# A hand-planned linear-attention and MLP kernel: other ready times for loaded rows, a last tile in two column halves, table copies as planned tasks

## The chip, the cores and the metric

The kernel runs on one core of a Trainium2 chip. Its time is the device time of one launch in microseconds (us). The core has five engines that each work through their own instructions in order: TensorE (PE in the profile; its weight loads are PEld), VectorE (DVE), ScalarE (ACT), GpSimd (POOL) and SyncE (SP). Sixteen DMA engines move data between memory and the core; the kernel starts transfers from the queues of SyncE, ScalarE and GpSimd. TensorE writes to PSUM, eight banks of 2 KB per partition; everything else lies in SBUF.

## What is computed

A recurrent linear attention (RWKV-5) for 4 sequences of 768 steps with 8 heads of 48 columns, then a normalised two-layer MLP with a residual, over 384 columns:

```python
def _attn_ref(r, k, v, w, u):
    state = np.zeros((B, H, D, D), dtype=np.float32)
    for t in range(S):
        cur = np.einsum('bhd,bhe->bhde', u[None] * kt, vt)
        y[:, :, t] = np.einsum('bhd,bhde->bhe', rt, state + cur)
        state = w[None, :, :, None] * state + np.einsum('bhd,bhe->bhde', kt, vt)

def _moe_ref(x, g_ln, w_ch1, w_ch2):
    xn = (x - mu) / np.sqrt(var + 1e-06) * g_ln
    ch = np.maximum(xn @ w_ch1, 0.0) @ w_ch2
    return x + ch
```

All inputs and the output are float32. The hidden layer has 1536 columns.

## The kernel before

The 4 x 768 rows are cut into 24 tiles of 128 rows, six for each sequence. Inside a tile the recurrence is written as matmuls. Row t of r is scaled by w^t and row t of k by w^-t, so that decayed scores are a plain product, masked to the lower triangle; the state that goes from a tile to the next is multiplied by w^128. The scaling factors are three tables, Fr (two halves, for the even and the odd rows that r's load puts side by side) and Fk.

For tile i, with the planner's task names: sck scales k and scr scales a pair of r tiles (L366, L369), TK and TR transpose them on TensorE through the one PSUM bank "tr" (L384, L399), kT and rT copy them out (L388, L404), q is their product (L415) and cc the bonus sums by matmul (L442), copied out by cp (L453). "at" are the scores (L422), A the masked scores (L432), vc the cast of v to bf16 (L375), Vb the bonus term (L457), kv, S and Z the state (L473, L488, L497), y the output of the attention (L513, L525), x that with its row sum (L538). xn, sq and rs centre the rows and make the scale of the normalisation (L556, L565, L576). ln or a DMA transpose turns xn (L602, L610), lc copies it out of PSUM for the first eight tiles (L614). Then come the MLP's up matmuls (L627) for a group of one tile (the first six) or two tiles, re, the rectifier on ScalarE or VectorE (L641, L643), the down matmuls dn (L654), ot, the final sum (L664), and st, the store (L675). dn of a tile has 12 matmuls of 384 columns in three tasks of four; they add up in bank "o", or in one of the two "hp" banks for the odd ones of the last four tiles.

Which engine does what and in which order is set by a planner that runs when the kernel is built (class Planner, L22). Each task has an engine, a cost in us, tasks that it needs, buffers that it takes and gives, a priority, and perhaps other engines with their costs (alt). The planner holds a clock for each engine. Again and again it takes the task that can start first, on the engine on which it would end first, and writes its instructions there. A load has a planned landing, made from one planned DMA clock: it starts at most 3 us before that clock, moves it by `load`, and lands `lands` (1.9 us unless given) later. The planned times are used for the order alone; on the chip an instruction waits for its data, and everything behind it on its engine waits with it.

Line 74 of the planner adds SLK to ready times of TensorE's tasks, and SLK is 0.0, so it adds nothing. PACE = 4.4 holds the scaling of k: from the seventh tile on it is planned no sooner than 35 us + 4.4 us for each tile (L730).

The start is written by hand: the powers of w are made on VectorE by scans, transposed on TensorE (L308), and the three tables copied by ScalarE (L310). To the planner this is three tasks without instructions, "scan", "Fr" and "Fk", that only stand for the time. While TensorE has nothing to do in the first stage, keep_warm (L266) writes matmuls without use into bank "o" for the gap that the planner sees (L816 to L820).

The loads go in the order of `seq` (L697), with three loads of w1 behind the ninth and three of w2 behind the fourteenth. There are 7 buffers each for k, v and the cast v, 4 for pairs of r, 2 for scaled r, 4 for scaled k, 8 for the hidden layer hT, 11 for x.

Of the kernel before, what the change touches and what calls it, by code (L numbers as in the profile page):

```python
# [9 lines left out]
FP32 = mybir.dt.float32  # L10
# [7 lines left out]
SLK, SLT = 0.0, 35.0  # L18
# [3 lines left out]
class Planner:  # L22
# [24 lines left out]
    def order(self, patience=0.0, spread=0.0, seed=0):  # L47
# [15 lines left out]
        while todo:  # L63
            best = None
            for t in todo:
                data = t["after"]
                ok = True
                for n in t["needs"]:
                    d = self.by_name[n]
                    if d["end"] is None:  # L70
                        ok = False
                        break
                    lag = 0.0 if d["eng"] == t["eng"] else self.LAG[d["eng"]]
                    if t["eng"] == "PE" and d["eng"] not in ("PE", "") and eng_at["PE"] > SLT:
                        lag += SLK
                    data = max(data, d["end"] + lag)
# [50 lines left out]
def kernel(  # L127
# [16 lines left out]
    L = P  # L144
# [158 lines left out]
    LH = L // 2  # L303
    for j in range(3):
        fps = ps_h.tile([P, 512], FP32, name="hp") if j < 2 else ps.tile([P, 512], FP32, name="y")
        for kc in range(CK):
            src = T2[:, kc] if j == 2 else T[:, kc, j : 2 * L : 2]
            nc.tensor.transpose(out=fps[:, kc * P : (kc + 1) * P], in_=src, identity=ident_f[:])  # L308
        src = fps[:, :C].rearrange("p (h d) -> p h d", h=H)
        nc.scalar.copy(out=Fr[:, j] if j < 2 else Fk[:], in_=src)  # L310
# [89 lines left out]

    def evacuate_r(i, eng):
        e, c = divmod(i, 2)
        rT_t[i] = trp.tile([P, HP, P], BF16, name="rT", bufs=NRT)
        (eng.copy if eng is nc.scalar else eng.tensor_copy)(  # L404
            out=rT_t[i][:].rearrange("p q (t j) -> p q j t", j=2),
            in_=tp_t[e][:, :, c * LH : (c + 1) * LH].rearrange("p (j q) t -> p q j t", j=2),
        )
# [43 lines left out]
    def bonus_copy(i):  # L451
        cc_t[i] = sb2.tile([P, H], FP32, name="cc")
        nc.scalar.copy(out=cc_t[i][:], in_=s_t[i][:, C : C + H])  # L453
# [158 lines left out]
    def ln_evacuate(i):  # L612
        g, j = tile_group[i]
        nc.scalar.copy(out=xT_t[g][:, :, j * P : (j + 1) * P], in_=tp_t[i][:, :CK, :])  # L614
# [3 lines left out]
    def up(g, m):  # L618
        gw = group_len[g] * P
        nf = 512 // gw  # L620
        if m == 0:
            hT_t[g] = sb3.tile([P, FK, GW], BF16, name="hT", bufs=NH)
# [54 lines left out]

    plan = Planner(
# [5 lines left out]
    add("scan", "DVE", 5.65, None, pri=99)  # L684
    add("Fr", "ACT", 5.9, None, pri=99)
    add("Fk", "ACT", 0.65, None, needs=["Fr"], pri=99)
# [36 lines left out]
    for i in range(NT):  # L723
# [8 lines left out]
        if not half:  # L732
            add(f"scrb{e}", "", 0.0, None, [], [("scr", e, 1)], pri=p0)
            for t in range(2):
                add(f"scr{e}{t}", "POOL", 1.1, lambda g, e=e, t=t: scale_r(e, t, g), [f"r{e}", "Fr", f"scrb{e}"], [],
                    [("r", e)], pri=p0, alt=[("DVE", 0.7)])
            add(f"TR{e}", "PE", 0.46, lambda e=e: transposes_r(e), [f"scr{e}0", f"scr{e}1"], [("tr", ("r", e), 2)],
# [7 lines left out]
        else:  # L745
            add(f"kT{i}", "SP", 1.25, lambda i=i: transpose_k_by_dma(i), [f"sck{i}"], [("kT", i, 2)], [("sck", i)], pri=80,
                load=0.67, lands=3.0)
# [11 lines left out]
        add(f"cp{i}", "ACT", 0.2, lambda i=i: bonus_copy(i), [f"cc{i}"], [("cc", i, 1)], [("s", i)], pri=p0 + 1)  # L759
# [32 lines left out]
        if i < LNP:  # L792
            add(f"ln{i}", "PE", 0.18, lambda i=i: ln_transposes(i), [f"xn{i}", f"xT{g}"], [("tr", ("l", i), 1)],
                [("xn", i)], pri=p0 + 2)
            add(f"lc{i}", "ACT", 0.5, lambda i=i: ln_evacuate(i), [f"ln{i}"], [], [("tr", ("l", i))], pri=p0 + 2)
        else:
            add(f"lc{i}", "SP", 1.2, lambda i=i: ln_by_dma(i), [f"xn{i}", f"xT{g}"], [], [("xn", i)], pri=90, load=0.5, lands=3.0)
        for m in range(NM):
# [7 lines left out]
    for g, n in enumerate(group_len):  # L806
        for m in range(NU[g]):
# [3 lines left out]
                [f"lc{group_first[g] + j}" for j in range(n)] + [f"w1s{q}{kc}" for q in w for kc in range(CK)],  # L811
                [("hp", (g, m), 1)] + ([("hT", g, n)] if m == 0 else []), [("xT", g)], pri=-40, kind="u")
            add(f"re{g}_{m}", "ACT", 0.6, lambda e, g=g, m=m: relu(g, m, e), [f"up{g}_{m}"], [], [("hp", (g, m))], pri=30, alt=RA)
    pe_at = 6.1
# [39 lines left out]
```

## Time and profile before

| | |
|---|---|
| median of 13 runs | 158.27 us (156.98 to 160.22) |
| the profiled execution | 157.08 us |
| its span, first to last instruction | 155.3 us |
| granted TensorE clock, mean | 1.000 |
| TensorE busy | 146.4 us (94%) |
| VectorE busy | 119.1 us (77%) |
| ScalarE busy | 97.0 us (62%) |
| GpSimd busy | 85.8 us (55%) |
| moved by DMA | 25.46 MB, mean 164 GB/s |
| landing of the last v | 94.5 us |
| last attention matmul of the last tile (L525) | 122.6 us |
| last matmul | 151.5 us |
| last store: issue, landing | 152.21, 154.08 us |

The page of the profile is of that one execution. The 40 slices of a row each stand for 3.9 us, and a digit is the busy share in tenths. In the tables by stage each engine's busy us is followed by the number of its instructions, then come the granted clock, the share of the DMA engines and GB/s. In a timeline a line has start, duration, engine, line, operation, output and inputs, and in brackets how long the engine was idle before it and what ended that. In a list of waits a line has who waited for whom, us in total, how often, and the longest.

### The profile page before, as it was taken

The numbers are of one execution on the slowest core, as the hardware profiler recorded it, in microseconds if no ns is written. First come the engines' busy times: TensorE is split into PE (matmuls) and PEld (weight loads), VectorE is DVE, ScalarE is ACT, GpSimd is POOL, SyncE is SP. The second block draws the span as 40 slices with busy tenths as digits, with TensorE's granted clock in tenths as the row PEclk, the third lists the DMA queues.
The fourth block names the chain that finished last, engine by engine and source line by source line (L and its number), as shares of the span: only waits on it lengthen the run. The fifth ranks groups of instructions, "written<-read, shape, count | busy, mean of one in ns | idle before, by whom it ended". The sixth has DMA issues, their size and how long they took to land.

```text
span 155.3 us, 4634 instructions
## 1 busy us (share of the span) xinstructions
PE 146.4 (94%) x1851; PEld 114.7 (74%) x1851; DVE 119.1 (77%) x232; ACT 97.0 (62%) x217; POOL 85.8 (55%) x116
## 2 busy tenths in 40 slices
PE   5999999989999999999989989999999999999990
PEld 5889898867887667777758767787787777777650
DVE  5879999978898999999999879898989731101231
ACT  3568888867866577667858558676576554463100
POOL 7379697588729896785975939954442120000000
PEclk9999999999999999999999999999999999999999
DMA  4999999999999899899998977212121220111122
GB/s 94 235 239 336 353 195 287 367 226 214 243 222 214 207 234 226 192 231 172 227 222 178 204 175 157 78 30 76 50 55 51 80 73 3 51 55 51 51 101 101
DMA packets 75418, 25.46 MB, mean 164 GB/s; under 512 B 69632, under 2 KB 74246, under 8 KB 75398
## 3 DMA queue, kind: packets, MB, share of 16 engines
q1 hardware_dynamic: 72070, 23.21, 64.4%
q10 hardware_dynamic: 3232, 1.97, 4.2%
q8 instruction: 14, 0.23, 0.7%
q14 instruction: 6, 0.05, 0.1%
q0 software_dynamic: 96, 0.01, 0.0%
HBM read 18.88 MB, written 4.72 MB: 152 GB/s over the span
## 4 chain that ended last, share of the span: by engine, by line
PE 47%; DMA 21%; SPq 8%; DVE 7%; POOL 6%; issue 4%; ACT 4%; POOLq 0%; ACTq 0%
PE o L654 18%; PE hp L627 18%; DMA wst<-in_moe_w_ch_dram 11%; DMA v<-in_v_dram 10%; SPq L195 5%; PE hp L654 3%; DVE q L415 2%; PE at L422 2%; PE tr L399 2%; PE tr L384 1%; PE y L525 1%; POOL w_sb L350 1%; POOL Vb L457 1%; ACT kT L388 1%; DVE A L432 1%
## 5 line engine op out<-in xcount | busy, mean ns | idle before, releaser
L627 PE MATMUL hp<-xT,w_sb 128*128 128x256 bf16 (+1 forms) x540 | 57.6, 251 | 0.0
L654 PE MATMUL o<-w_sb,hT 128*128 128x384 bf16 x264 | 52.1, 326 | 0.0
L627 PEld LDWEIGHTS <-w_sb 128*128 128x128 bf16 x540 | 43.5, 98 | 7.2 <-DVE w_sb L350 0.2
L641 ACT ACTIVATE hT<-hp 128x512 bf16<-128x512 f32 x60 | 35.7, 598 | 19.1 <-PE hp L627 18.5
L654 PEld LDWEIGHTS <-hT 128*128 128x128 bf16 x288 | 26.2, 98 | 13.1
L664 DVE SCALAR_TENSOR_TENSOR ot<-o,rs,x 128x384 f32<-128x384 f32 x22 | 13.4, 610 | 22.5 <-PE o L654 22.5
L432 DVE TENSOR_TENSOR A<-at,mask 128x1024 bf16<-128x1024 f32 x24 | 29.1, 1214 | 0.5 <-PE at L422 0.5
L457 POOL TENSOR_TENSOR Vb<-v,cc 128x384 f32<-128x384 f32 x24 | 20.0, 835 | 11.2 <-ACT cc L453 11.2
L369 POOL TENSOR_TENSOR sc<-r,Fr 128x384 bf16<-128x384 f32 x18 | 20.2, 1134 | 6.3 <-ACT Fr L310 2.8
L366 POOL TENSOR_TENSOR sc<-k,Fk 128x384 bf16<-128x384 f32 x19 | 19.7, 1038 | 0.0
L388 ACT COPY kT<-tr 128x512 bf16<-128x512 bf16 x22 | 12.9, 586 | 5.5 <-PE tr L384 3.4
L565 ACT ACTIVATE sq<-x,sum 128x384 bf16<-128x384 f32 x24 | 14.6, 607 | 2.1 <-DVE x L538 2.1
L404 ACT COPY rT<-tr 128x512 bf16<-128x512 bf16 x17 | 11.8, 736 | 3.6 <-PE tr L399 2.3
L268 PE MATMUL o<-ident 128*128 128x128 bf16 x152 | 12.1, 233 | 1.6 <-DVE ident L243 1.6
L538 DVE SCALAR_TENSOR_TENSOR x<-y,Vb 128x384 f32<-128x384 f32 x24 | 13.1, 546 | 0.4 <-PE y L525 0.2
L268 PEld LDWEIGHTS <-ident 128*128 128x128 bf16 x152 | 9.9, 104 | 1.9 <-DVE ident L243 1.6
L422 PE MATMUL at<-rT,kT 48*128 48x128 bf16 x192 | 9.5, 219 | 1.2 <-ACT kT L388 1.1
L643 DVE TENSOR_SCALAR hT<-hp 128x512 bf16<-128x512 f32 x12 | 8.2, 687 | 2.0 <-PE hp L627 1.8
L525 PE MATMUL y<-vv,A 128*128 128x48 bf16 x192 | 8.8, 184 | 1.0 <-DVE A L432 1.0
L556 ACT ACTIVATE xn<-x,sum 128x384 bf16<-128x384 f32 x13 | 8.0, 615 | 2.6 <-DVE x L538 2.6
L497 DVE TENSOR_TENSOR Z<-S,WLZ 128x384 bf16<-128x384 f32 x11 | 9.4, 856 | 0.0
L422 PEld LDWEIGHTS <-kT 48*128 48x128 bf16 x192 | 5.4, 94 | 4.9 <-ACT kT L388 2.4
(87 smaller groups left out, 195.8 us busy)
## 6 DMA issues: line engine op xcount, KB each, us to landing
r<-in_r_dram SPq DMA_DIRECT2D x12, 384.0 KB, 4.7
k<-in_k_dram SPq DMA_DIRECT2D x24, 192.0 KB, 4.6
wst<-in_moe_w_ch_dram SPq DMA_DIRECT2D x6, 768.0 KB, 7.6
v<-in_v_dram SPq DMA_DIRECT2D x22, 192.0 KB, 4.0
out_dram<-ot SPq DMA_DIRECT2D x16, 192.0 KB, 3.3
out_dram<-ot ACTq DMA_DIRECT2D x8, 192.0 KB, 1.9
v<-in_v_dram ACTq DMA_DIRECT2D x2, 192.0 KB, 3.5
xT<-xn SPq DMA_TRANSPOSE x16, 3.0
```

The costliest lines, as they stand in the source:

```text
L268: nc.tensor.matmul(out=warm[:, :P], lhsT=ident[:], rhs=ident[:], start=True, stop=True)
L366: eng.tensor_tensor(out=k_bufs[i % NSC][:, :, :D], in0=k_t[i][:], in1=Fk[:], op=ALU.mult)
L369: eng.tensor_tensor(out=r_bufs[e % NSR][:, j, :, :D], in0=r_t[e][:, :, j * D : (j + 1) * D], in1=Fr[:, j], op=ALU.mult)
L388: (eng.copy if eng is nc.scalar else eng.tensor_copy)(out=kT_t[i][:], in_=tk_t[i][:, :HP, :])
L422: nc.tensor.matmul(out=at_t[i][:, par, p, :], lhsT=kT_t[i][p0 : p0 + D, p, :], rhs=rT_t[i][p0 : p0 + D, p, :], start=True, stop=True,)
L432: nc.vector.tensor_tensor(out=A_t[i][:].rearrange("p e q t -> p (e q) t"), in0=at_t[i][:].rearrange("p e q t -> p (e q) t"), in1=mask[:].u ...
L457: nc.gpsimd.tensor_tensor(out=Vb_t[i][:], in0=vf_t[i][:], in1=cc_t[i][:].unsqueeze(2).to_broadcast([P, H, D]), op=ALU.mult)
L565: nc.scalar.activation(out=sq[:], in_=x_t[i][:], func=ACT.Square, bias=sum_t[i][:], scale=-float(C), accum_out=sq_t[e][:, c : c + 1],)
L627: nc.tensor.matmul(out=hp[:, f * gw : (f + 1) * gw], lhsT=w1_sb[:, n, kc, fb * P : (fb + 1) * P], rhs=xT_t[g][:, kc, :gw], start=(kc == 0) ...
L641: nc.scalar.activation(out=out, in_=src, func=ACT.Relu)
L654: nc.tensor.matmul(out=o_t[i][:, :C], lhsT=hT_t[g][:, fk, j * P : (j + 1) * P], rhs=w2_sb[:, fk, :], start=(fk == 0), stop=(fk == FK - 1),)
L664: nc.vector.scalar_tensor_tensor(out=ot_t[i][:], in0=o_t[i][:, :C], scalar=rs_t[i // 2][:, i % 2 : i % 2 + 1], in1=x_t[i][:], op0=ALU.mult ...
```

## The change

There are five edits.

1. SLK, SLT go from 0.0, 35.0 to 3.0, 30.0, and the rule that they stand in is another one. It no longer looks at TensorE. Now any task with an engine that needs a load of the common kind (`lands` is 1.9: r, k, v, w1, w2) whose planned start is over 30 us is ready 3.0 us later than that load's planned landing.
2. The three tables are copied by planned tasks Fr0, Fr1 and Fk, each on ScalarE (0.5) or VectorE (0.48). Place-holders "first" and "rows0" stand for the time of ScalarE and GpSimd before, and tFr0, tFr1 and tFk for the ends of the transposes. scr of each half needs its own half of Fr.
3. The last tile's down matmuls are 2 x 12 of 192 columns, in two column halves with an "hp" bank each, the second after the first; each half has its own final sum and store.
4. cp (0.2 on ScalarE) may go to VectorE at 0.15, lc (0.5) at 0.36. TR needs the TK of the tile before, from the eleventh tile on.
5. A place-holder hTb takes the hidden layer's buffer as soon as a group's rows are there; before, the first up task took it. `up` makes the tile when it is first wanted. The place where the planner's clock of TensorE begins for keep_warm goes from 6.1 to 6.3. A `lands` of 5.0 in place of 3.0 is in a branch for tiles from KP = 24 on, of which there are none.

```diff
-SLK, SLT = 0.0, 35.0
+SLK, SLT = 3.0, 30.0
...
-                    if t["eng"] == "PE" and d["eng"] not in ("PE", "") and eng_at["PE"] > SLT:
+                    if d["load"] and d["lands"] == 1.9 and t["eng"] and d["start"] > SLT:
                         lag += SLK
...
-        fps = ps_h.tile([P, 512], FP32, name="hp") if j < 2 else ps.tile([P, 512], FP32, name="y")
+        tab.append(ps_h.tile([P, 512], FP32, name="hp") if j < 2 else ps.tile([P, 512], FP32, name="y"))
...
-        src = fps[:, :C].rearrange("p (h d) -> p h d", h=H)
-        nc.scalar.copy(out=Fr[:, j] if j < 2 else Fk[:], in_=src)
+
+    def copy_table(j, eng):
+        src = tab[j][:, :C].rearrange("p (h d) -> p h d", h=H)
+        (eng.copy if eng is nc.scalar else eng.tensor_copy)(out=Fr[:, j] if j < 2 else Fk[:], in_=src)
...
-        if m == 0:
+        if g not in hT_t:
             hT_t[g] = sb3.tile([P, FK, GW], BF16, name="hT", bufs=NH)
...
+    def down_half(h, m):
+        g, j = tile_group[NT - 1]
+        if m == 0:
+            oh_t[h] = ps_h.tile([P, 512], FP32, name="hp")
+        for fk in range(m * PM, (m + 1) * PM):
+            nc.tensor.matmul(
+                out=oh_t[h][:, :CH],
+                lhsT=hT_t[g][:, fk, j * P : (j + 1) * P],
+                rhs=w2_sb[:, fk, h * CH : (h + 1) * CH],
+                start=(fk == 0),
+                stop=(fk == FK - 1),
+            )
+
+    def finish_half(h):
+        i = NT - 1
+        oth_t[h] = sb2.tile([P, CH], FP32, name="oth")
+        nc.vector.scalar_tensor_tensor(
+            out=oth_t[h][:],
+            in0=oh_t[h][:, :CH],
+            scalar=rs_t[i // 2][:, i % 2 : i % 2 + 1],
+            in1=x_t[i][:, h * CH : (h + 1) * CH],
...
+    def store_half(h, eng):
+        b, c = divmod(NT - 1, NCH)
+        eng.dma_start(out=out[b, c * L : (c + 1) * L, h * CH : (h + 1) * CH], in_=oth_t[h][:])
...
-    add("scan", "DVE", 5.65, None, pri=99)
-    add("Fr", "ACT", 5.9, None, pri=99)
-    add("Fk", "ACT", 0.65, None, needs=["Fr"], pri=99)
+    add("scan", "DVE", 5.75, None, pri=99)
+    add("first", "ACT", 4.95, None, pri=99)
+    add("rows0", "POOL", 4.9, None, pri=99)
+    for j, (name, done, bank_) in enumerate((("Fr0", 5.45, "hp"), ("Fr1", 5.85, "hp"), ("Fk", 6.2, "y"))):
+        add(f"t{name}", "", done, None, pri=99, takes=[(bank_, ("t", j), 1)])
+        add(name, "ACT", 0.5, lambda e, j=j: copy_table(j, e), [f"t{name}"], gives=[(bank_, ("t", j))], pri=99 - j, alt=[("DVE", 0.48)])
...
-                add(f"scr{e}{t}", "POOL", 1.1, lambda g, e=e, t=t: scale_r(e, t, g), [f"r{e}", "Fr", f"scrb{e}"], [],
+                add(f"scr{e}{t}", "POOL", 1.1, lambda g, e=e, t=t: scale_r(e, t, g), [f"r{e}", f"Fr{t}", f"scrb{e}"], [],
...
-            add(f"TR{e}", "PE", 0.46, lambda e=e: transposes_r(e), [f"scr{e}0", f"scr{e}1"], [("tr", ("r", e), 2)],
+            add(f"TR{e}", "PE", 0.46, lambda e=e: transposes_r(e), [f"scr{e}0", f"scr{e}1"] + ([f"TK{i - 1}"] if QP < i < KP else []), [("tr", ("r", e), 2)],
...
-        add(f"cp{i}", "ACT", 0.2, lambda i=i: bonus_copy(i), [f"cc{i}"], [("cc", i, 1)], [("s", i)], pri=p0 + 1)
+        add(f"cp{i}", "ACT", 0.2, lambda e, i=i: bonus_copy(i, e), [f"cc{i}"], [("cc", i, 1)], [("s", i)], pri=p0 + 1, alt=[("DVE", 0.15)])
...
+        if i == NT - 1:
+            for h in range(2):
+                for m in range(NM):
+                    add(f"dh{h}{m}", "PE", 0.34, lambda h=h, m=m: down_half(h, m),
+                        [f"re{g}_{u}" for u in range(NU[g])] + ([f"dh{h}{m - 1}"] if m else [f"dh0{NM - 1}"] if h else []),
+                        [("hp", ("oh", h), 1)] if m == 0 else [], [("hT", g)] if m == NM - 1 and h else [], pri=-40, kind="d")
+                add(f"oh{h}", "DVE", 0.38, lambda h=h: finish_half(h), [f"dh{h}{NM - 1}", f"rs{i // 2}"], [],
+                    [("hp", ("oh", h))] + ([("x", i)] if h else []), pri=99)
+                add(f"sh{h}", "SP", 0.55, lambda e, h=h: store_half(h, e), [f"oh{h}"], pri=99, load=0.3, lands=1.8,
+                    alt=[("ACT", 0.5)])
+            continue
...
+        add(f"hTb{g}", "", 0.0, None, rows_in, [("hT", g, n)], pri=-40)
...
-    pe_at = 6.1
+    pe_at = 6.3
```

## The prediction

> **What bounds the kernel now.** I read the page's 40 slices first, then a table of busy time by stage, then TensorE's timeline from start to start, then the waits of the other engines, and last the stores.
>
> ```profile
> PE   5999999989999999999989989999999999999990
> ...
> DVE  5879999978898999999999879898989731101231
> ...
> PEclk9999999999999999999999999999999999999999
> DMA  4999999999999899899998977212121220111122
> ```
>
> TensorE is busy in every slice, at the full granted clock, and the DMA engines are busy until about 92 us. "Busy" alone proves little, so I went by start times. In the last 55 us four matmuls of 384 columns take 0.65 us from start to start (162 ns each), six of 256 columns 0.655 (109 each), twelve of 128 columns 0.67 (56 each). At these steps the MLP alone is 288 x 162 + 324 x 109 + 216 x 56 ns = 94.1 us of 155.3. Adding up, from 16.8 us on, what start-to-start times hold beyond such steps leaves only some 9 us, of which some 4 are two short joints of about 0.1 us around each tile's scores (L422). The rest are a dozen stalls: 0.52 us at 24.3, 0.91 at 32.7, 0.45 at 51.4, 0.52 at 55.5, 0.23 at 60.6 and at 75.6, 0.49 at 79.8, 0.54 at 81.0, 0.84 at 89.9, and smaller ones. After 97 us there is hardly one. So the end is TensorE's queue of work plus the stalls in front of it, and then a tail.
>
> ```profile
> core 0: us, PE busy (x) PEld busy (x) DVE busy (x) ACT busy (x) POOL busy (x), PEclk, DMA share, GB/s
> 16.00:34.00 18.00, 16.87 (x300) 14.58 (x298) 16.64 (x32) 14.73 (x33) 13.88 (x20) 1.00 1.04 287
> 34.00:50.00 16.00, 15.96 (x240) 12.85 (x237) 14.14 (x26) 12.30 (x29) 10.70 (x14) 1.00 1.02 221
> 50.00:70.00 20.00, 19.31 (x241) 14.31 (x239) 20.00 (x37) 13.54 (x33) 16.29 (x20) 1.00 0.99 220
> 70.00:92.00 22.00, 20.54 (x279) 15.70 (x278) 20.00 (x37) 15.53 (x38) 15.97 (x21) 1.00 1.00 197
> ```
>
> From 50 to 92 us VectorE has 2 us free in 42: most stalls there are TensorE waiting for VectorE's A or q. One is a different thing, and it is the kind that the change is about:
>
> ```profile
> 89.65 0.51 ACT L375 CAST vv<-v 128x384 bf16<-128x384 f32 x1 [1.79 <-DMA v<-in_v_dram]
> 90.07 0.16 ACT L453 COPY cc<-s 128x8 f32<-128x8 f32 x1
> 90.13 0.59 ACT L388 COPY kT<-tr 128x512 bf16<-128x512 bf16 x1
> ```
>
> ```profile
> 89.72 0.36 PE L525 MATMUL y<-vv,A 128*128 128x48 bf16 x8
> 90.77 0.40 PE L422 MATMUL at<-rT,kT 48*128 48x128 bf16 x8 [0.69 <-ACT kT L388]
> ```
>
> ScalarE stands 1.79 us in front of a cast of v that nobody needs soon; the copies cc and kT queue behind it, and TensorE, which needs kT, stands from 89.93 to 90.77. In all:
>
> ```profile
> ACT vv L375 <- DMA v<-in_v_dram: 2.9, 3, 1.8
> ...
> POOL vv L375 <- DMA v<-in_v_dram: 3.9, 5, 1.9
> ```
>
> **Part 1, the lag of 3 us on loaded rows.** It adds no instruction. In the planner every task that needs r, k or v, where the load's planned start is over 30 us, is treated as if its data came 3 us later, so others are put ahead of it in each engine's order. It can remove the 2.9 us of ScalarE, 3.9 of GpSimd and 0.3 of VectorE above. The scalings of k and r hardly wait for DMA after 34 us (0.2 us once), so nothing is won there. On TensorE's path I count the 0.84 us at 89.9 in full. The chain of waits also runs from a load of v (65.24, 3.80 us) through ScalarE's cast at 69.06, sq, hT, kT and rT to the 0.23 us at 75.6: I count 0.2. With 4.9 us of waits in 50 to 92 us gone, ScalarE and GpSimd can take work that the planner's choice by earliest finish now gives to VectorE (xn costs it 0.4 to 0.88 there); the two stalls behind VectorE at 79.8 and 81.0 are 1.03 us: between 0 and 1.03, I take 0.4, nearer the end at which VectorE stays full. Sum -1.4 us, bounds 0 and -2.1.
>
> What does the lag cost? The cast is needed by kv and y: the v that lands at 89.6 is read after 110 us. From the sixth pair of r on, 7 to 20 us lie between scaling (53.5 us for the r that landed at 53.20) and transposing (64.7). Only at the seam is it close: the r that landed at 34.74 is transposed at 36.45, and its scores start at 42.23, so 3 us are hidden by those 5.8 and by MLP of the first six tiles: of its 18 groups up and 18 down, 11 and 3 have run by 35 us, and 7 x 0.67 + 15 x 0.65 = 14.4 us are left. Without that cover it costs 3 us. Buffers: an r buffer is refilled 18 us after its scaling (done by 50.8, load at 68.2); v's is held by Vb longer than by the cast; k's is paced by PACE. So loads on SyncE's queue need not move: 0, with the whole 3 us as bound.
>
> **Part 2, the re-plan.** A list planner that has other ready times gives another order everywhere after them. I can bound this only: stalls over the joints after 24 us are 5.3 us in this plan, of which 2.1 are in part 1's bound; what is left, 3.2, could go, or come once more. Half of it either way, +-1.6, is my spread, 0 what I take. Of the moved choices: cp may go to VectorE (0.16 us by its copy of 11 columns at L321, against 0.164 on ScalarE), lc likewise (0.41 us by its 512-column copy at L388 as upper bound, against 0.471, eight of them before 53 us). TR after the previous TK is already the order on TensorE from the eleventh tile on (85.79, 88.03, then 91.86): 0. The hT place-holder and the check on hT_t issue nothing: 0, hidden by eight hT buffers.
>
> **Part 3, the tables.** Now three copies on ScalarE, 0.98 for two and 0.48, from 5.46 to 6.82 us. By the new costs the second goes to VectorE, which ends its scans at 5.72 and must then scale r (0.56) and k (1.08): Fr1 there is 0.48 more before sc. Fr0 is no sooner, Fk at best 0.1 sooner. First k scaled: 6.86 now, 6.9 to 7.4 then. The cover is that the first up matmul, at 16.77, waits for w1, whose load lands at 15.69; after it VectorE is full, so some may come through: 0 to +0.4, I take +0.1. A pe_at later by 0.2 drops some four warm-up matmuls of 56 ns where TensorE idles anyway: 0.
>
> **Part 4, two halves of the last tile.**
>
> ```profile
> 150.06 1.46 PE L654 MATMUL hp<-w_sb,hT 128*128 128x384 bf16 x8
> ...
> 151.56 0.62 DVE L664 SCALAR_TENSOR_TENSOR ot<-hp,rs,x 128x384 f32<-128x384 f32 x1 [0.62 <-PE hp L654]
> ```
>
> The tail is 0.62 of finish, a store issued at 152.21 that lands at 154.08, and 1.22 us of closing. Removed: 12 matmuls of 384 columns, 1.95 us. Added: 24 of 192; between 56 ns at 128 and 109 at 256 columns that is 82, 1.98 us, so +0.03. The page "TensorE: Matmul & The Clock Gate", section "Back-to-back issue gap", speaks against this part: it gives streams that reload weights for each matmul about 81 ns at 128 columns, so narrow ones pay for their weights. By it 24 narrower matmuls would take at least 24 x 81 = 1.94 us, an estimate, and would have no room to be cheaper than the wide ones; this trace runs 128 columns in 56, and so the row is used. A finish of 192 columns costs between half (0.31) and, from the slope between 384 columns at 0.61 and 1024 at 1.21 (0.94 ns each), 0.43: I take 0.38, -0.24. The half store moves 96 KB; a 192 KB one took 1.81 to 1.87 us from issue to landing on idle DMA engines, and its packets spread over 0.65 us: between 0 and -0.33, I take -0.15, as latency is the bigger share. The page "DMA: Bandwidth & Descriptors", section "Anatomy of one DMA", puts about 2.0 us of a DMA down as fixed and the rest at 436 GB/s; an estimate by it is -0.23. The first half's finish and store lie under the second's 1.0 us of matmuls; its extra issue (0.34 on ScalarE's empty queue, or SyncE's) is off the end. Were the halves placed ahead of the 23rd tile, the tail would be as now. The second half needs a second hp bank, freed by the 22nd tile's finish; behind it on TensorE stands nothing but the end. Sum -0.36, bounds +0.03 and -0.6.
>
> **Sum.** -1.4 + 0 + 0.1 - 0.36 = -1.7 us: span 155.3 to 153.6. The profiled execution took 157.08 with a span of 155.3, 1.19 under the median 158.27; I carry the difference to the median: **156.6**. Own range: the parts' bounds stand above the taken values by 1.4, 1.6, 0.3 and 0.4, below them by 0.7, 1.6, 0.1 and 0.2; as root sums 2.2 and 1.8, so 154.8 to 158.8.
>
> **Rivals.** *VectorE pays (slower).* cp and casts go to VectorE where it has 2 us free in 42. About ten tiles pass there: 10 x 0.16 for cp, and five casts of v more at 0.44, is 3.8 us; less the 2.0 free, 1.8 on the path, and the waits removed from others no longer matter; with part 4, 155.3 + 1.8 + 0.1 - 0.36 = 156.8, at the median 159.8. It decides as soon as VectorE's added work from 50 to 92 exceeds its 2 us free. For it: the planner weighs finishing times, not VectorE's slowing beside GpSimd (Z takes 0.54 or 1.35). Against it: greedy choice goes to VectorE only when it comes free first. *Nothing moves but the tail (same).* The stalls go elsewhere, since each wait on DMA had other work waiting too, or the lag tests planned times that miss the late loads: -0.36 + 0.1, 158.0. For it: only one stall of nine is DMA's directly. *The seam starves (slower).* The 3 us at 35 are not filled: 155.3 + 3 - 1.7 = 156.6, at the median 159.5; against it the 14.4 us of MLP.
>
> **Chances.** Forecast 0.66, VectorE 0.13, tail alone 0.14, seam 0.07. Faster or slower means by over 0.5%, about what a measurement of this kernel can tell from no change: under 157.5, over 159.1. Of the forecast 0.57 is faster and 0.09 the same; of the tail alone 0.04, 0.08 and 0.02 slower; the other two are slower. Together faster 0.61, same 0.17, slower 0.22. The range goes up to 159.6, which takes in the tail alone, the seam and part of VectorE's case, and down to 154.3, between the root sum's 154.8 and all lower bounds at once, 154.0.
>
> **What would show it.** Right: casts of v wait under 1 us for DMA in all; no stall near 89.9; stalls after 34 us sum to under 3 us beyond the joints; a tail near 3.4 us from the last matmul's end, not 3.8; 24 matmuls of 192 columns at about 82 ns. Wrong: VectorE at 20.00 in 50 to 70 and later with more stalls behind A and q, a hole near 40 us, or a down matmul of the 23rd tile last.

## The result, and the profile after

The changed kernel is slower. Its median is 160.41 us (158.96 to 162.68, 11 runs) against 158.7 us for the kernel before, run on the same chip (156.64 to 161.36, 48 runs); the ratio is 1.0122, with a 95% interval of 1.0081 to 1.0163. The forecast was 156.6 us, with a range up to 159.6. Ratios here and below compare, for each kernel, the runs within 1.5% of its fastest, so they are not quotients of the medians.

The profiled execution of the changed kernel took 158.97 us with a span of 156.9 (before: 157.08 and 155.3). These are the same four rows of the 40 slices:

```profile
PE   5999998989999999986999999999999999999991
DVE  5889679689879897999899999997988841011141
PEclk9999999999999999999999999999999999999999
DMA  4999999999999899999998997332112121111122
```

TensorE is again busy nearly everywhere (the 8 and the 6 around 70 us are new), at the full granted clock. The table of busy time by stage (columns as in the table shown for the kernel before) says what the change did to VectorE:

```profile
50.00:70.00 20.00, 19.26 (x263) 14.97 (x262) 18.15 (x37) 14.57 (x33) 17.56 (x22) 1.00 1.03 219
70.00:92.00 22.00, 20.68 (x272) 16.32 (x271) 20.77 (x40) 16.62 (x37) 14.95 (x20) 1.00 1.12 195
```

VectorE has 18.15 us in the stage in which it had 20.00, and 20.77 where it had 20.00; it is no worse off than before. The waits for the DMA queues that the change aims at have shrunk too. Each line is who waited for whom, us in total, how often, the longest:

```profile
ACT vv L379 <- DMA v<-in_v_dram: 1.5, 1, 1.5
POOL vv L379 <- DMA v<-in_v_dram: 0.7, 1, 0.7
PE hp L632 <- DMA xT<-xn: 0.6, 1, 0.6
```

The casts of v wait 2.2 us where they waited 7.1. The third line is new: TensorE itself waits for a DMA.

And the end. This is VectorE's timeline with the last store:

```profile
153.67 0.42 DVE L702 SCALAR_TENSOR_TENSOR oth<-hp,rs,x 128x192 f32<-128x192 f32 x1 [0.32 <-PE hp L691]
154.12 0.34 ACTq L713 DMA_DIRECT2D out_dram<-oth  x1
```

The last matmul ends at 153.64. A finish of 192 columns takes 0.42 us against 0.62, and the half store that closes the run is issued at 154.12. From the last matmul's end to the end of the span are now 3.28 us, before 3.78. So the tail gives 0.5 us, and yet the span is 1.6 longer: the last matmul ends 2.1 us later. What TensorE did in that time can be added up in the two traces:

| from before to after, us | |
|---|---|
| matmuls of keep_warm, 152 to 195: 43 x 56 ns | +2.4 |
| stalls beyond the usual start-to-start steps, 12.8 to 12.4 in all | -0.3 |
| 24 matmuls of 192 columns (83 ns each) for 12 of 384 (162 ns) | +0.03 |
| sum, to set beside the last matmul's +2.1 | +2.1 |
| tail | -0.5 |
| span | +1.6 |

The matmuls of keep_warm in the two traces, before and after (form, count, min/median/max of the duration in ns, first and last start in us):

```profile
L268 PE MATMUL o<-ident x152: 219/219/314, 1.6 to 28.8; 128*128 128x128 bf16 x152
```

```profile
L268 PE MATMUL o<-ident x195: 216/219/314, 1.6 to 29.0; 128*128 128x128 bf16 x195
```

The loss is not a stall that a list of waits would show. It is matmuls without use, all before 30 us, and so in a part of the run that the lag, which begins at 30 us of planned time, cannot reach. VectorE's timeline at the start shows where they come from. First the kernel before, then after:

```profile
5.97 0.56 DVE L369 TENSOR_TENSOR sc<-r,Fr 128x384 bf16<-128x384 f32 x1 [0.26 <-ACT Fr L310]
...
11.97 0.55 DVE L538 SCALAR_TENSOR_TENSOR x<-y,Vb 128x384 f32<-128x384 f32 x1
...
12.92 1.21 DVE L432 TENSOR_TENSOR A<-at,mask 128x1024 bf16<-128x1024 f32 x1
```

```profile
6.11 0.56 DVE L313 COPY Fr<-hp 128x384 f32<-128x384 f32 x1 [0.39 <-PE hp L309]
6.58 0.55 DVE L373 TENSOR_TENSOR sc<-r,Fr 128x384 bf16<-128x384 f32 x1
...
12.76 1.21 DVE L437 TENSOR_TENSOR A<-at,mask 128x1024 bf16<-128x1024 f32 x1
...
13.89 0.54 DVE L543 SCALAR_TENSOR_TENSOR x<-y,Vb 128x384 f32<-128x384 f32 x1
```

The second table's copy now stands on VectorE and puts its scaling of r from 5.97 to 6.58. That alone is 0.6 us. But two tasks have changed places behind it: x of the first tile came before A of the second, and now comes after it, at 13.89 in place of 11.97. What follows stands on TensorE's timeline, before and after:

```profile
13.49 0.33 PE L602 MATMUL tr<-ident,xn 128*128 128x128 bf16 x3
...
15.54 0.61 PE L399 MATMUL tr<-ident,sc 128*128 128x128 bf16 x8
...
17.74 0.40 PE L422 MATMUL at<-rT,kT 48*128 48x128 bf16 x8
...
23.50 0.33 PE L602 MATMUL tr<-ident,xn 128*128 128x128 bf16 x3
```

```profile
16.50 0.33 PE L607 MATMUL tr<-ident,xn 128*128 128x128 bf16 x3
...
17.71 0.33 PE L607 MATMUL tr<-ident,xn 128*128 128x128 bf16 x3
17.87 0.83 PE L632 MATMUL hp<-xT,w_sb 128*128 128x128 bf16 x12
...
19.49 0.61 PE L403 MATMUL tr<-ident,sc 128*128 128x128 bf16 x8
...
21.48 0.40 PE L427 MATMUL at<-rT,kT 48*128 48x128 bf16 x8
...
26.30 1.17 PE L268 MATMUL o<-ident 128*128 128x128 bf16 x18
27.68 0.55 PE L268 MATMUL o<-ident 128*128 128x128 bf16 x7
28.14 0.33 PE L607 MATMUL tr<-ident,xn 128*128 128x128 bf16 x3
28.30 0.89 PE L268 MATMUL o<-ident 128*128 128x128 bf16 x13
```

The lines with three matmuls into tr are the transposes of xn (ln), those with eight into tr from sc the transposes of a pair of r (TR). Both take the one PSUM bank "tr", as TK does. Before, ln of the first tile was through at 13.5 and TR of the second pair followed at 15.54. After, xn of the first tile is late because x is late; ln of the first tile goes at 16.50, ln of the second at 17.71, and only then, at 19.49, TR of the second pair. The third tile's scores move from 17.74 to 21.48, ln of the third tile from 23.50 to 28.14. TensorE has no rows for its next up matmuls in between and runs 18 + 7 + 13 matmuls of keep_warm from 26.30 on.

Of the 43 more in all, 23 stand after 24 us, where the third tile's rows are missing. Another 19 stand ahead of the first up matmul: it starts at 17.87 instead of 16.77, because the rows of the first tile are copied out of bank "tr" only from 17.31 to 17.65. These matmuls fill time in which TensorE's next task has no data: ln at 28.14, for one, starts when bank "tr" is free, at 28.09. That they are a filling and not themselves the cause is read from such lines; no run left them out.

### The profile page after: what moved, and what is told of

The parts are those of the page before. It is cut to its first block, busy times and chain, and to the rows that moved or that the text cites. A ratio compares the mean times of both kernels' runs of the same rounds, so it can differ in the third digit from the quotient of the medians.

```text
span 156.9 us, 4742 instructions
## 1 busy us (share of the span) xinstructions
PE 148.7 (95%) x1906; PEld 119.0 (76%) x1906; DVE 117.4 (75%) x243; ACT 95.7 (61%) x207; POOL 87.4 (56%) x116
## 3 DMA queue, kind: packets, MB, share of 16 engines
q1 hardware_dynamic: 73254, 23.50, 67.2%
## 4 chain that ended last, share of the span: by engine, by line
PE 69%; DMA 11%; DVE 8%; SPq 5%; issue 2%; ACT 2%; DVEq 0%
PE hp L632 26%; PE o L659 24%; DMA wst<-in_moe_w_ch_dram 9%; SPq L195 4%; PE at L427 4%; DMA xT<-xn 3%; PE tr L388 2%; PE tr L403 2%; DVE A L437 2%; PE y L530 2%; PE s L478 2%; PE s L447 2%; PE y L518 1%; PE hp L691 1%; PE hp L659 1%
## 5 line engine op out<-in xcount | busy, mean ns | idle before, releaser
L659 PE MATMUL o<-w_sb,hT 128*128 128x384 bf16 x264 | 52.7, 326 | 0.1
L659 PEld LDWEIGHTS <-hT 128*128 128x128 bf16 x276 | 25.4, 98 | 11.3 <-issue 0.3
L669 DVE SCALAR_TENSOR_TENSOR ot<-o,rs,x 128x384 f32<-128x384 f32 x22 | 13.5, 614 | 22.6 <-PE o L659 22.5
L370 POOL TENSOR_TENSOR sc<-k,Fk 128x384 bf16<-128x384 f32 x18 | 18.6, 1038 | 0.0
L268 PE MATMUL o<-ident 128*128 128x128 bf16 x195 | 15.0, 231 | 1.6 <-DVE ident L243 1.6
L392 ACT COPY kT<-tr 128x512 bf16<-128x512 bf16 x22 | 12.8, 584 | 4.5 <-PE tr L388 2.5
L268 PEld LDWEIGHTS <-ident 128*128 128x128 bf16 x195 | 12.4, 104 | 2.0 <-DVE ident L243 1.6
L409 ACT COPY rT<-tr 128x512 bf16<-128x512 bf16 x14 | 10.0, 731 | 3.2 <-DVE rT L409 1.7
L581 POOL TENSOR_SCALAR rs<-sqs 128x2 f32<-128x2 f32 x12 | 2.3, 193 | 14.5 <-ACT sq L570 14.2
L379 ACT CAST vv<-v 128x384 bf16<-128x384 f32 x18 | 9.2, 512 | 1.5 <-DMA v<-in_v_dram 1.5
L584 POOL TENSOR_TENSOR rs<-rs,expo 128x2 f32<-128x2 f32 x12 | 8.4, 702 | 1.0
L388 PE MATMUL tr<-ident,sc 128*128 128x128 bf16 x92 | 8.9, 219 | 0.0
```

The source lines that it names most:

```text
L268: nc.tensor.matmul(out=warm[:, :P], lhsT=ident[:], rhs=ident[:], start=True, stop=True)
L370: eng.tensor_tensor(out=k_bufs[i % NSC][:, :, :D], in0=k_t[i][:], in1=Fk[:], op=ALU.mult)
L659: nc.tensor.matmul(out=o_t[i][:, :C], lhsT=hT_t[g][:, fk, j * P : (j + 1) * P], rhs=w2_sb[:, fk, :], start=(fk == 0), stop=(fk == FK - 1),)
L669: nc.vector.scalar_tensor_tensor(out=ot_t[i][:], in0=o_t[i][:, :C], scalar=rs_t[i // 2][:, i % 2 : i % 2 + 1], in1=x_t[i][:], op0=ALU.mult ...
```

## The experiments

Two theories stood against each other. **Tables:** the loss lies in part 3, through the new order in bank tr; the lag does what it should. **Lag:** the re-plan behind the lag costs the time, and the start is made up for later, since TensorE has idle time to spare there. Single executions of one kernel differ by some us (before: 156.6 to 161.4), so verdicts go by ratios, and profiles are read for order, waits and clock. In the tables below H stands for the halves, T for the planned tables, C for the edits to cp, lc, TR and the hT place-holder, and L for the lag.

### Halves alone, and the halves again

The kernel before, with the halves only (functions and tasks as in the change; both runs are of one kernel):

```diff
+        if i == NT - 1:
+            for h in range(2):
+                for m in range(NM):
+                    add(f"dh{h}{m}", "PE", 0.34, lambda h=h, m=m: down_half(h, m),
...
+            continue
```

> The kernel before with the last tile's two column halves alone; everything ahead of the last 12 us keeps its order. Theory (the loss is made in the first 30 us by the planned table copies, the halves are a small gain): span about 154.8, 0.5 under 155.3, 152 warm-up matmuls as before, ratio to before near 0.997. Rival (the halves cost TensorE time at the end): span over 155.5.

> The kernel before with the halves alone once more, as the measure for the two kernels with the lag on casts: ratio to before 0.99 to 0.998, span 154.8 to 157; the casts of v wait 7 us or more for DMA.

Measured: 0.9906 [0.9852, 0.9959] the first time, 0.9951 [0.9910, 0.9992] the second. These are 1.5 and 0.8 us won; the intervals reach from 0.1 to 2.3, so part 4 wins by itself. The forecast's 0.36 us and the 0.5 us of the changed kernel's tail lie within the second interval, and below the first, which begins at 0.65. The medians of all runs differ by less, 159.00 against 159.17 and 158.44 against 159.10, so the size of the gain is not settled. Both profiled executions took 160.3 us, so the forecast spans were not seen in a profile; in them the casts of v wait 14.3 and 12.8 us.

### The lag alone

```diff
-SLK, SLT = 0.0, 35.0
+SLK, SLT = 3.0, 30.0
...
-                    if t["eng"] == "PE" and d["eng"] not in ("PE", "") and eng_at["PE"] > SLT:
+                    if d["load"] and d["lands"] == 1.9 and t["eng"] and d["start"] > SLT:
```

> The kernel before with the lag of 3 us on loaded rows alone. Theory (lag is no cost): first up matmul at 16.8 us and 152 warm-up matmuls as before, casts of v wait under 3 us for DMA instead of 7.1, span 154.3 to 155.5. Rival (the lag delays attention at 35 us and crowds it later): span 156.5 or more, with stalls between 35 and 100 us that sum to 1.2 us or more above before's.

Measured: 1.0294 [1.0233, 1.0356]. The start is as before (152 matmuls of keep_warm, first up matmul at 17.1), the casts of v wait for no DMA at all, and it is the slower for it by 4.7 us. On TensorE's timeline:

```profile
80.13 0.38 PE L384 MATMUL tr<-ident,sc 128*128 128x128 bf16 x4 [1.12 <-POOL Z L497]
...
83.12 1.46 PE L627 MATMUL hp<-xT,w_sb 128*128 128x256 bf16 x6 [2.61 <-DMA xT<-xn]
```

Here the MLP has run out. TensorE waits for the transposed rows of a two-tile group, whose DMA was issued at 78.72 and landed at 83.1. The stages around it:

```profile
78.00:80.00 2.00, 1.01 (x17) 0.77 (x16) 1.70 (x4) 2.00 (x6) 1.75 (x2) 1.00 1.03 200
80.00:82.00 2.00, 0.38 (x4) 0.21 (x3) 1.98 (x6) 1.25 (x3) 1.51 (x3) 0.79 1.19 276
82.00:84.00 2.00, 0.88 (x5) 0.64 (x6) 0.20 (x1) 0.20 (x2) 0.89 (x2) 0.50 1.28 192
84.00:86.00 2.00, 2.00 (x24) 1.40 (x23) 1.38 (x2) 0.17 (x1) 0.01 (x1) 0.50 1.14 221
86.00:88.00 2.00, 2.00 (x9) 1.09 (x8) 2.00 (x4) 1.00 (x2) 1.78 (x2) 0.50 1.15 223
88.00:90.00 2.00, 2.00 (x37) 1.57 (x35) 0.68 (x4) 0.60 (x1) 0.00 (x0) 1.00 0.75 150
```

The granted clock (the third number from the end) falls from 1.00 to 0.50 and stays there until 88: from 84 to 88 TensorE is busy in full and starts 33 matmuls in 4 us, where the last line has 37 in 2 us (part of that is their shapes). The hole is paid twice.

### The hole filled

Is the clock a real share of that? The same kernel, with 44 matmuls without use put ahead of the up matmuls that stand behind the hole:

```diff
+        if (g, m) == (8, 0):
+            for _ in range(44):
+                nc.tensor.matmul(out=hp[:, :P], lhsT=ident[:], rhs=ident[:], start=True, stop=True)
```

> The lag alone, as in the run that took 162.2 us, with 44 matmuls without use (56 ns each, 2.5 us) written ahead of the third two-tile group's first up matmul, into the bank that it then overwrites; there TensorE stood 2.6 us for the DMA transposition of xn, and its clock was granted at 0.50 from 81.6 to 88. Theory (the stall's second price is the clock): the granted clock stays at 1.00 from 76 to 94 us, the wait for xn is no shorter, span 159.5 to 160.5, about 2 us less. Rival (only the missing data counts): span 161.5 to 163.

Measured: 1.0153 [1.0096, 1.0210]. The stages:

```profile
78.00:80.00 2.00, 1.02 (x19) 1.02 (x19) 1.78 (x5) 1.25 (x4) 2.00 (x3) 1.00 1.13 316
80.00:82.00 2.00, 2.00 (x37) 1.97 (x35) 1.06 (x2) 1.04 (x3) 1.16 (x3) 1.00 0.88 176
82.00:84.00 2.00, 2.00 (x31) 1.41 (x29) 1.49 (x2) 0.73 (x3) 0.59 (x2) 1.00 0.87 175
```

The clock stays at 1.00, the rows still land late (81.2 us; the up matmuls start at 81.7), and 1.4% of the 2.9% is gone: the clock was about 2.2 us of the loss. What is left, 1.5% or 2.4 us, is about the length of the hole, which the 44 matmuls now fill (44 x 56 ns = 2.5 us). So work without use made this kernel faster.

### The tables undone

The changed kernel, with the tables copied by hand as before:

```diff
-    add("scan", "DVE", 5.75, None, pri=99)
...
-        add(name, "ACT", 0.5, lambda e, j=j: copy_table(j, e), [f"t{name}"], gives=[(bank_, ("t", j))], pri=99 - j, alt=[("DVE", 0.48)])
+    add("scan", "DVE", 5.65, None, pri=99)
+    for j in range(3):
+        copy_table(j, nc.scalar)
+    add("Fr", "ACT", 5.9, None, pri=99)
+    add("Fk", "ACT", 0.65, None, needs=["Fr"], pri=99)
```

> The changed kernel with the three table copies by hand on ScalarE and their old place-holders; lag, halves and the copies cc and xT on either engine stay. Theory: TR of the second r pair stands ahead of the second tile's ln again, first up matmul near 16.8 instead of 17.9, warm-up matmuls near 152 instead of 195, span 154.0 to 155.3. Rival (lag or the copies on VectorE make the loss): span 156.3 to 157.2, as with the whole change.

Measured: 0.9972 [0.9922, 1.0023]. Against the changed kernel's 1.0122 that is 1.5%, or 2.4 us. That this equals the 43 matmuls of the budget above is in part luck, since behind 30 us the two kernels have different stalls. The trace has 151 of them, TR of the second pair at 15.7, the first up matmul at 17.3. For "tables" this is the main evidence; "lag" had the loss stay. The profile also shows why it is no faster than before: a stall of 1.95 us at 66.4 for transposed rows (issued at 64.4, landed at 68.3), and the clock behind it:

```profile
66.00:68.00 2.00, 0.37 (x8) 0.26 (x8) 1.39 (x5) 1.19 (x3) 1.21 (x3) 1.00 1.02 228
68.00:70.00 2.00, 1.59 (x10) 1.25 (x11) 1.15 (x1) 0.12 (x1) 2.00 (x2) 0.55 1.14 213
70.00:72.00 2.00, 2.00 (x12) 1.23 (x11) 0.89 (x2) 1.67 (x4) 0.00 (x1) 0.60 0.94 231
72.00:74.00 2.00, 2.00 (x30) 1.41 (x29) 1.67 (x2) 0.90 (x3) 0.66 (x1) 1.00 0.86 196
```

Not every run of this kernel paid for the clock: the four with a mean granted clock of 0.998 or more took 157.6 to 159.4 us (median 157.9), the six with 0.979 to 0.989 took 158.4 to 161.7 (median 159.7).

### The order in bank tr alone

If the order is the cause, it must cost the same without any table: the kernel before, where TR of the second pair has to wait for the second tile's ln copy.

```diff
-            add(f"TR{e}", "PE", 0.46, lambda e=e: transposes_r(e), [f"scr{e}0", f"scr{e}1"], [("tr", ("r", e), 2)],
+            add(f"TR{e}", "PE", 0.46, lambda e=e: transposes_r(e), [f"scr{e}0", f"scr{e}1"] + (["lc1"] if e == 1 else []), [("tr", ("r", e), 2)],
```

> The kernel before with one more need: TR of the second r pair waits for the second tile's lc, which is the order that the changed kernel has in bank tr; tables by hand, no lag, no halves. Theory: third tile's scores move from 17.7 to about 21 us, up matmuls are missing between 24 and 30 us, 175 warm-up matmuls or more, span 157 to 159. Rival (a later third tile is hidden by what the MLP has to do): span 155 to 156.

Measured: 1.0207 [1.0143, 1.0270]. The first up matmul is at 17.1, as without the edit; only TR moves, to 18.9, and with it the third tile's scores, to 20.8. The matmuls of keep_warm in this kernel, then in the one with the tables undone:

```profile
L268 PE MATMUL o<-ident x186: 216/219/314, 1.6 to 29.4; 128*128 128x128 bf16 x186
```

```profile
L268 PE MATMUL o<-ident x151: 216/219/314, 1.6 to 29.1; 128*128 128x128 bf16 x151
```

34 x 56 ns = 1.9 us more than the 152 of the kernel before, and 2.07% of 158.7 is 3.3 us: the order explains more than half of this kernel's loss by these matmuls alone. The rest lies in an order that is different behind 34 us, and it was not taken apart. All but four of the 34 stand behind the first up matmul, so this run shows the price of a late TR and late third tile; the late first tile of the changed kernel was not made on its own.

### The lag undone

```diff
-SLK, SLT = 3.0, 30.0
+SLK, SLT = 0.0, 30.0
```

> The changed kernel with SLK = 0, all else as changed. Theory: the first 30 us stay as in the changed kernel (first up at 17.9 us, some 195 warm-up matmuls), span 156.5 to 157.5. Rival (the lag costs): span 155.0 to 155.8.

Measured: 1.0323 [1.0234, 1.0412]. So in the changed kernel the lag is worth 2.0%, though alone it costs 2.9%. (The profiled execution took 169.27 us, far above this kernel's median of 164.67; only its count of matmuls is used below.)

### Tables and halves; copies and halves

Two of three taken out of the changed kernel. First no lag, and cp and lc on ScalarE only (T + H):

```diff
-SLK, SLT = 3.0, 30.0
+SLK, SLT = 0.0, 30.0
...
-        add(f"cp{i}", "ACT", 0.2, lambda e, i=i: bonus_copy(i, e), [f"cc{i}"], [("cc", i, 1)], [("s", i)], pri=p0 + 1, alt=[("DVE", 0.15)])
+        add(f"cp{i}", "ACT", 0.2, lambda e, i=i: bonus_copy(i, e), [f"cc{i}"], [("cc", i, 1)], [("s", i)], pri=p0 + 1, alt=[])
```

(lc in the same way.)

> The changed kernel without the lag and with cp and lc on ScalarE alone: table tasks and halves are left. Theory (the planned table copies put tile 0 some 0.45 us later and with that TR of the second r pair behind the lns): third tile's scores near 21 us instead of 17.7, 180 warm-up matmuls or more, span 157.5 or more. Rival (the tables do harm only with the copies on VectorE): span 155.5 or less.

Then no lag, and the tables by hand as above (C + H):

> The changed kernel without the lag and with the tables by hand: cp and lc on either engine, and the halves, are left. Theory: the first 30 us in the order of before, some 152 warm-up matmuls, span 154 to 156. Rival (the copies on a full VectorE cost, my recorded slower case): span 157 or more, stalls behind A and q.

Measured: T + H 1.0292 [1.0205, 1.0379], C + H 1.0035 [0.9993, 1.0077]. With the tables, 195 matmuls of keep_warm and the third tile's scores at 20.5; without them 151 and 18.0. The tables cost some 3 to 4% where there is no lag (1.0323 against 1.0035 with the copies, 1.0292 against the halves' 0.9951 and 0.9906). The order on VectorE goes with the tables and not with cp: in T + H, where cp is on ScalarE, A of the second tile starts at 12.56 and x of the first at 13.69; in C + H x stands first, at 11.99, and A at 12.94.

The copies cost 0.8 to 1.3% by the ratios against the halves alone (1.0035 beside 0.9951 and 0.9906), with intervals that only just stand apart. VectorE is not fuller by them: from 50 to 70 and 70 to 92 us it is busy for 17.62 and 18.26 us, before for 20.00 each. The three largest stalls of C + H behind 34 us have three causes: 1.64 us at 86.2 (behind ScalarE, whose cast stood 2.43 us for its load), 1.11 at 48.0 (behind VectorE's ot) and 1.07 at 78.2 (transposed rows). Its casts wait

```profile
ACT vv L379 <- DMA v<-in_v_dram: 6.3, 4, 2.4
POOL vv L379 <- DMA v<-in_v_dram: 5.5, 3, 3.1
```

11.8 us for their loads. With the tables undone, which is this kernel with the lag, they wait 0.3 us, and the ratio is 0.9972 against 1.0035: here the lag takes away nearly all of the waits and wins 0.6%, with intervals that overlap. T + H has only 3.2 us of such waits and is slow all the same: its largest stalls are 1.75 us at 51.6, until VectorE's ot has emptied bank "o", and 1.63 at 71.4, for transposed rows.

### The lag for one kind of task

Which of the tasks that read loaded rows must not be put off? The kernel before with the halves, and the lag for the scalings of k and r only, or for the casts of v only:

```diff
+                    if d["load"] and d["lands"] == 1.9 and t["eng"] and d["start"] > SLT and t["name"][:2] == "sc":
```

```diff
+                    if d["load"] and d["lands"] == 1.9 and t["eng"] and d["start"] > SLT and t["name"][:2] == "vc":
```

> The kernel before with the halves, and with the lag of 3 us on the scalings of k and r alone, not on the casts. Theory: attention is behind from 35 us on, TensorE runs out of MLP work between 65 and 90 us and waits for the DMA transposition of xn as with the whole lag, and the casts wait for DMA besides (7 us or more): ratio 1.02 or more, span 159 or more. Rival (the harm is at the casts): span 155.5 or less.

> The kernel before with the halves, and with the lag of 3 us on the casts of v alone, not on the scalings of k and r. Theory (the waits for loads are at the casts, the harm of the lag is at the scalings, which hold up the attention): casts wait under 3 us for DMA, TR of the fourth r pair no later than in the kernel before (36.5 us), no hole near 80 us, span 153.5 to 155.5, ratio 0.975 to 0.992. Rival (any new order of this planner loses about as much): span 157 or more.

Measured: scalings 1.0291 [1.0207, 1.0375], casts 0.9981 [0.9950, 1.0011]. The first has the lag's whole loss, though with the halves' gain in it. Here is TR of the fifth pair of r in three kernels: before, with the scalings put off, and with the casts put off:

```profile
43.81 0.61 PE L399 MATMUL tr<-ident,sc 128*128 128x128 bf16 x8
```

```profile
49.55 0.61 PE L399 MATMUL tr<-ident,sc 128*128 128x128 bf16 x8
```

```profile
44.22 0.61 PE L399 MATMUL tr<-ident,sc 128*128 128x128 bf16 x8
```

A lag of 3 us on paper put this TR 5.7 us later on the chip, and the ninth tile's y with it (its end at 59.3; with the casts put off 52.5, before 52.3). With the scalings put off TensorE has a hole of 2.61 us at 81.2, for transposed rows again (issued at 79.37, landed at 83.73), and in this execution the clock did not fall behind it:

```profile
82.00:84.00 2.00, 0.13 (x2) 0.15 (x3) 0.98 (x4) 2.00 (x7) 1.75 (x2) 1.00 1.16 167
```

So this kernel loses as much as the lag alone without that price in its profile; its other runs had mean clocks of 0.989, 0.989 and 0.979. The casts wait as badly as ever:

```profile
ACT vv L375 <- DMA v<-in_v_dram: 8.6, 7, 2.2
POOL vv L375 <- DMA v<-in_v_dram: 4.2, 2, 2.7
DVE vv L375 <- DMA v<-in_v_dram: 3.8, 3, 3.0
```

The lag for the casts takes these to 1.8 us and hardly moves r. But it was expected to win beyond the halves, and did not: 0.9981 stands above both runs of the halves alone. Its profile has a stall of 1.74 us at 88.6 for transposed rows, and a tail of 3.69 us: in this order twelve down matmuls of another tile stand behind the halves, so the end is nearly as long as with a whole last tile (3.78) and most of the halves' gain is gone. The prediction had named that case.

### The casts with 4 us

The same rule with a longer lag, the candidate for a kernel that beats both:

```diff
-SLK, SLT = 3.0, 30.0
+SLK, SLT = 4.0, 30.0
```

> As with the lag on casts alone, with 4 us in place of 3. Theory (what counts is that the casts stand behind the landing, not the 3 us): casts wait under 2 us, span 153.5 to 155.5, ratio 0.975 to 0.992. Rival (each value makes another order, with holes of its own): more than 1.5 us away from the 3 us one.

Measured: 0.9927 [0.9889, 0.9964], just above the forecast ratio, the casts waiting for no load (but the scalings 5.4 us for r, 0.2 before), TR of the fifth pair at 44.50, a tail of 3.32 us, the clock at 1.000. It is faster than the kernel before by 0.7% and than the changed one by 1.9% (0.9927 / 1.0122). But the halves alone (0.9906, 0.9951) do as well: that putting off the casts wins anything beyond them is not shown, neither with 3 us, which stands above both, nor with 4, which stands between them.

### All of them

| kernel | ratio to before, 95% | keep_warm matmuls |
|---|---|---|
| H | 0.9906 [0.9852, 0.9959]; 0.9951 [0.9910, 0.9992] | 152 |
| H, casts put off 4 us | 0.9927 [0.9889, 0.9964] | 152 |
| H + C + L (tables undone) | 0.9972 [0.9922, 1.0023] | 151 |
| H, casts put off 3 us | 0.9981 [0.9950, 1.0011] | 152 |
| H + C | 1.0035 [0.9993, 1.0077] | 151 |
| H + T + C + L, the change | 1.0122 [1.0081, 1.0163] | 195 |
| L, hole filled | 1.0153 [1.0096, 1.0210] | 152 |
| TR of the second pair late | 1.0207 [1.0143, 1.0270] | 186 |
| H, scalings put off 3 us | 1.0291 [1.0207, 1.0375] | 152 |
| H + T | 1.0292 [1.0205, 1.0379] | 195 |
| L | 1.0294 [1.0233, 1.0356] | 152 |
| H + T + C (lag undone) | 1.0323 [1.0234, 1.0412] | 195 |

The parts do not add up alike in every order. Along the one path on which each step was measured (H, then C, L and T), the steps are -0.5 to -0.9%, +0.8 to +1.3%, -0.6% (not settled) and +1.5%; the forecast had -0.2%, 0, -0.9% and +0.1%. T costs 1.5% beside the lag and 3 to 4% without it; L costs 2.9% in the old order, gives 0.6% (not settled) beside the halves and copies, and 2.0% with the tables too.

## Why the prediction was wrong

**The step that failed is part 3**, "0 to +0.4, I take +0.1", with the cover "that the first up matmul, at 16.77, waits for w1". The sizes in it were right: the second copy went to VectorE, and the first k was scaled at 7.26, within "6.9 to 7.4". The cover failed at its own place: the first up matmul moved from 16.8 to 17.9, because the rows of the first tile now came later than w1, and 1.1 us is above the part's bound of 0.4. It was also asked of the wrong thing. What the planned copies changed was not only a start time but the order of x and A on VectorE, and through it who gets bank tr first; the attention of the third tile fell 3.7 us back, and from 24 us on TensorE had no rows for the MLP. The +0.1 should have been about +2.4: shown by the changed kernel's budget, by the tables undone and, for the late TR, by the order in bank tr made late on its own. Part 2 was the place where an order was allowed to change, and it took 0 +-1.6 only for what lies behind 24 us; a re-plan ahead of 24 us was not in the sum at all. The same part put cp, lc, TR's need and the hT place-holder at 0; together they cost 0.8 to 1.3%, 1.3 to 2 us, in one pair of comparisons, and no run separates them. This is the second term that was mis-sized.

**Part 1** was right in what it removes and wrong in what it hides behind. The casts' waits went from 7.1 to 2.2 us; the mark set was under 1 us. Of the stalls behind 34 us 4.1 us became 3.1 (each over 0.13 us), so the gain on TensorE's path is about 1.0, not 1.4. On the cost side the prediction looked at the fourth pair of r and at those "from the sixth pair of r on", and passed over the fifth: it lands at about 40 us and is transposed at 43.81, so it has 4 us, not "7 to 20". And the "14.4 us" of MLP left at 35 us were counted as cover for what comes at 42 only. They are all that stands between the seam and the groups of two tiles, and TensorE uses them up: before, the second such group's rows land at 67.0 and its up matmuls start at 67.7, in the changed kernel both stand at 72.2. From there on anything that is late in the attention is late on TensorE. For the lag alone "The seam starves", at 0.07 the least likely of the list, was therefore the rival with the right mechanism, late scalings that starve the MLP; it had the hole near 40 us, and the runs have it at 66 to 83 us. For the whole change it is wrong too: there the lag wins 2.0%, and rows are missing at 26 us, from the tables.

**Part 4** was right: 83 ns for 192 columns (82 forecast), 0.42 us for the finish (0.38 forecast, near the upper bound of 0.43), 1.62 us from issue to landing for the last half store where a whole one took 1.85 to 1.88, so -0.23 and not -0.15 (the first half store, on SyncE's queue, took 1.83). The prediction's estimate by the page "DMA: Bandwidth & Descriptors", section "Anatomy of one DMA", was -0.23 too, though that section's fit is for transfers that GpSimd issues and these went by other queues. In sum +0.03 - 0.20 - 0.23 = -0.4 against -0.36, where the tail as a whole gave -0.5. On the page "TensorE: Matmul & The Clock Gate", section "Back-to-back issue gap", the prediction set a rule of 81 ns for 128 columns aside for the trace's 56; the changed kernel's trace again has 56 there.

**VectorE pays** is false for the change: 18.15 and 20.77 us of VectorE in the two stages, where it was to be full; that its 159.8 us lies near the measured 160.41 is luck. **Nothing moves but the tail** is false too, since the matmuls' end moved by +2.1.

A last weakness was in the base. The profile of the kernel before shows 7.1 us of waiting casts; in orders without the lag on casts other profiles have 3.2 (T + H), 11.8 (C + H), 13.6 (TR late), 16.6 (scalings put off) and, with the halves alone, 14.3 and 12.8. What the lag on casts can win changes with the order by more than the prediction's whole spread, and was read from one execution.

Open: why the tables cost about twice as much without the lag as beside it, since T + H hardly waits for casts; what in cp and lc costs; why a hole costs the clock in one run and not in another; and whether the lag on casts wins anything beside the halves.

## What to carry to other kernels

When a ready time or a cost changes in a kernel whose order is planned, compare the order of the tasks around each single buffer first (here one PSUM bank), from the start of the run on: half a microsecond can turn two tasks round and cost five times as much, far away. Slack for late loads belongs to the consumer, not to the load: here a cast that nobody needs for 20 us can be put off and a scaling on the way to the next scores cannot. And backlog is spent once: a cover counts only if it is still there when the next late thing arrives.

## What the runs showed of the hardware

The granted clock can fall after holes that are short, and need not. In the kernel with the lag alone the holes were 1.28 and 2.77 us with 0.4 us of matmuls between them, and the clock was at 0.50 from 81.2 to 88.0 us; with the tables undone a hole of 1.95 us, with little but eight short matmuls in the 0.7 us ahead of it, brought 0.50 from 68.2 to 71.6. With the hole filled it stayed at 1.00 and the run was 1.4% shorter. But with the scalings put off a hole of 2.61 us left it at 1.00, and so did one of 1.74 us with the casts put off 3 us. One kernel differs from run to run: with the tables undone the mean granted clock of ten runs lay between 0.979 and 1.000.

The page "TensorE: Matmul & The Clock Gate", section "Why this matters for your kernels", allows idle gaps up to about 3 us before the rate halves. The hole of 1.95 us above does not fit that, and the measurement decides; the hole of 2.61 us that left the clock at 1.00 does fit it. Length alone does not separate them here.

The DMA transposes of rows took 2.3 us from issue to landing on quiet DMA engines and, among loads, up to 5.5 (with the scalings put off) and 4.4 at the hole of the lag alone (78.72 to 83.1); where TensorE has nothing else ready, that difference is a hole.
